# A decode block on one core: one tile program with a rolled load loop, and five engine programs with their own semaphores

## The chip, the cores and the metric

One core of a Trainium2 chip runs the kernel; the other cores have nothing to do with it. The metric is the device time of one execution in microseconds. The profile is one further execution, recorded by the hardware profiler.

## The reference

One token of width 640 passes a transformer block: layer norm, attention over a cache of 8192 positions with 32 heads of width 192, a residual, layer norm again, a gated FFN with ReLU, a residual. All data are 32-bit floats. The two caches are 201 MB each and by far the largest inputs.

```python
def reference(A_x, A_k_cache, A_v_cache, A_wq, A_wo, B_x, B_W_gate, B_W_up, B_W_down):
    # B, Sq, D = 1, 1, 640; H, Sk, Dh = 32, 8192, 192; F = 1536
    q = (layernorm(x) @ wq).reshape(B, Sq, H, Dh).transpose(0, 2, 1, 3)
    p = softmax(einsum("bhqd,bhkd->bhqk", q, k_cache) * (Dh ** -0.5))
    o = einsum("bhqk,bhkd->bhqd", p, v_cache)
    h = x + o.transpose(0, 2, 1, 3).reshape(B, Sq, H * Dh) @ wo
    n = layernorm(h)
    gate = n @ W_gate
    return h + ((gate * (gate > 0)) * (n @ W_up)) @ W_down
```

The excerpt joins the two blocks of the reference and leaves out its helper functions.

## The kernel before

The host packs, for every head, one array of keys (`kq`) and one of values (`vo`), each 128 partitions by 13248 floats, so that one transfer of 6.78 MB brings a head's K with its query weights, and another its V with its output weights. The transfers all go through the load queue that SyncE (SP) feeds.

There is one buffer for K (`kp`, `k_t`) and there are two for V (`vp`, `v_t`). A head is two functions. `keys` computes the head's query with five matmuls from the weights behind K (line 156), picks its components out with two reductions on VectorE (`ttr`, line 148), spreads them over columns with two scalings on ScalarE (lines 164 and 165), and forms the scores with 24 matmuls of 512 columns (line 171), each of which the profile shows as two passes. Then come the maximum (lines 174 to 178), the exponential (line 181) and the reciprocal of its sum (line 185). `values` multiplies V with the probabilities in twelve VectorE instructions of 1024 columns, each with its sum over the row (line 148 again), adds up with TensorE (line 195), scales, and adds the head's part of the output projection to the accumulator `acc` in PSUM, where it stays over all heads (lines 203 and 205).

Thirty heads run in a loop, two heads in each turn (`For_i`, line 213); the last two stand behind it, and the last V comes in four pieces. `manual_schedule` keeps each engine's instructions in the order of the program text: the query of a head stands behind the values of the head before on TensorE, and each wait is derived from the buffers by the tile framework. At the end of the loop the engines meet at a barrier. The FFN's weights go into the K buffer and one V buffer, in the load queue behind the last V (lines 232 to 236). The FFN itself is lines 238 to 287: row sums of the accumulator on ScalarE (242), the statistics, the up and gate projections (266), the ReLU product and its transpose (276, 278), the down projection (283), the residual (286), the store (287).

Of the kernel before, what the change touches and what calls it, by code (L numbers as in the profile page):

```python
# [15 lines left out]
NG = 8  # L16
# [3 lines left out]
QB = 512  # L20
D1 = P
D2 = DH - P
KW = S + S // 2
WW = DH * D // P
TW = KW + WW
# [4 lines left out]
@with_exitstack  # L30
def kernel(
    ctx: ExitStack,
    tc: tile.TileContext,
    x: bass.AP,
    kq: bass.AP,
    vo: bass.AP,
    w_gate: bass.AP,
    w_up: bass.AP,
    w_down: bass.AP,
    out: bass.AP,  # L40
):
    nc = tc.nc
    DG = D // NQ
    FG = F // NQ

    const = ctx.enter_context(tc.tile_pool(name="const", bufs=1))
    kp = ctx.enter_context(tc.tile_pool(name="kp", bufs=1))
    vp = ctx.enter_context(tc.tile_pool(name="vp", bufs=2))
    pp = ctx.enter_context(tc.tile_pool(name="pp", bufs=2))
    small = ctx.enter_context(tc.tile_pool(name="small", bufs=2))  # L50
    row = ctx.enter_context(tc.tile_pool(name="row", bufs=1))
    ps_s = ctx.enter_context(tc.tile_pool(name="ps_s", bufs=1, space=bass.MemoryType.PSUM))
    ps_q = ctx.enter_context(tc.tile_pool(name="ps_q", bufs=2, space=bass.MemoryType.PSUM))
    ps_m = ctx.enter_context(tc.tile_pool(name="ps_m", bufs=2, space=bass.MemoryType.PSUM))
    ps_a = ctx.enter_context(tc.tile_pool(name="ps_a", bufs=1, space=bass.MemoryType.PSUM))
    ctx.enter_context(tc.manual_schedule())

    xT = const.tile([P, DJ], F32, name="xT")
    nc.sync.dma_start(xT, x[0, 0].rearrange("(p j) -> p j", p=P))

    def load_k(h):
        t = kp.tile([P, TW], F32, name="k_t")
        nc.sync.dma_start(t, kq[h])
        return t

    def load_v(h, parts):
        t = vp.tile([P, TW], F32, name="v_t")
        b = 0
        for n in parts:
            nc.sync.dma_start(t[:, b:b + n], vo[h][:, b:b + n])  # L70
            b += n
        return t

    xrow = const.tile([1, D], F32, name="xrow")
    nc.scalar.dma_start(xrow, x[0])

    ones = const.tile([P, P], F32, name="ones")
    nc.gpsimd.memset(ones, 1.0)
    share = const.tile([P, P], F32, name="share")
    nc.gpsimd.memset(share, 1.0 / C)  # L80
    eps = const.tile([P, 1], F32, name="eps")
    nc.gpsimd.memset(eps, EPS)
    ident = const.tile([P, P], F32, name="ident")
    from concourse.masks import make_identity
    make_identity(nc, ident)

    def fold(name, n, view):
        t = const.tile([P, n], F32, name=name)
        nc.vector.reduce_sum(t, view, axis=AX.X)
        return t  # L90

    low = fold("low", D2, ident.rearrange("p (a f) -> p f a", f=D2))
    same = const.tile([P, NG, C], F32, name="same")
    nc.vector.reduce_sum(same[:, 0, :], ident.rearrange("p (a c) -> p c a", c=C), axis=AX.X)
    nc.vector.tensor_copy(same[:, 1:NG, :], same[:, 0:1, :].to_broadcast([P, NG - 1, C]))
    blk = fold("blk", NG, ident.rearrange("p (a c) -> p a c", c=C))
    blk2 = fold("blk2", NJ - NG, low.rearrange("p (a c) -> p a c", c=C))
    half = fold("half", 2, ident.rearrange("p (a c) -> p a c", c=D2))
    side = const.tile([P, 2, D2], F32, name="side")
    nc.vector.tensor_copy(side, half[:, :, None].to_broadcast([P, 2, D2]))  # L100
    pick = const.tile([P, 3, 2, C], F32, name="pick")
    nc.gpsimd.memset(pick, 0.0)
    for i in range(2):
        nc.gpsimd.memset(pick[:, i, i, :], 1.0)
    nc.vector.tensor_copy(pick[:, 2], half[:, :, None].to_broadcast([P, 2, C]))

    def rstd_of(dst, var, name):

        ve = const.tile([P, 1], F32, name=f"ve{name}")
        nc.vector.tensor_scalar_add(ve, var, EPS)  # L110
        sd = const.tile([P, 1], F32, name=f"sd{name}")
        nc.scalar.activation(sd, var, AF.Sqrt, bias=eps)
        y = const.tile([P, 1], F32, name=f"y{name}")
        nc.vector.reciprocal(y, sd)
        t = const.tile([P, 1], F32, name=f"t{name}")
        nc.vector.scalar_tensor_tensor(t, y, ve, y, op0=ALU.mult, op1=ALU.mult)
        nc.vector.tensor_scalar(t, t, -0.5, 1.5, op0=ALU.mult, op1=ALU.add)
        nc.vector.tensor_mul(dst, y, t)

    s1 = const.tile([P, 1], F32, name="s1")  # L120
    nc.vector.reduce_sum(s1, xT, axis=AX.X)
    pm = ps_m.tile([P, QB], F32, name="ps_small")
    nc.tensor.matmul(pm[:, 0:1], ones, s1, start=True, stop=True)
    mean = const.tile([P, 1], F32, name="mean")
    nc.vector.tensor_scalar_mul(mean, pm[:, 0:1], 1.0 / D)
    xc = const.tile([P, DJ], F32, name="xc")
    nc.vector.tensor_scalar(xc, xT, mean, None, op0=ALU.subtract)
    xsq = const.tile([P, DJ], F32, name="xsq")
    nc.vector.tensor_mul(xsq, xc, xc)
    s2 = const.tile([P, 1], F32, name="s2")  # L130
    nc.vector.reduce_sum(s2, xsq, axis=AX.X)
    pv = ps_m.tile([P, QB], F32, name="ps_small")
    nc.tensor.matmul(pv[:, 0:1], ones, s2, start=True, stop=True)
    var = const.tile([P, 1], F32, name="var")
    nc.vector.tensor_scalar_mul(var, pv[:, 0:1], 1.0 / D)
    rstd = const.tile([P, 1], F32, name="rstd")
    rstd_of(rstd, var, "x")
    xn = const.tile([P, DJ], F32, name="xn")
    nc.vector.tensor_scalar_mul(xn, xc, rstd)

    HN = D // 2
    acc = ps_a.tile([P, HN], F32, name="acc")
    for i in range(2):
        nc.tensor.matmul(acc[i * D2:(i + 1) * D2, :], ones[0:1, 0:D2], xrow[:, i * HN:(i + 1) * HN],
                         start=True, stop=False, skip_group_check=True)

    def ttr(dst, a, b, scale, out):
        nc.vector.tensor_tensor_reduce(out=out, in0=a, in1=b, scale=scale, scalar=0.0,  # L148
                                       op0=ALU.mult, op1=ALU.add, accum_out=dst)

    def keys(kt):

        wq = kt[:, KW:TW].rearrange("p (j n) -> p j n", n=DH)
        pq = ps_q.tile([P, QB], F32, name="pq")
        for j in range(DJ):
            nc.tensor.matmul(pq[:, 0:DH], xn[:, j:j + 1].to_broadcast([P, P]), wq[:, j, :],  # L156
                             start=(j == 0), stop=(j == DJ - 1))
        q = small.tile([P, 2], F32, name="q")
        junk = small.tile([P, DH], F32, name="junk")
        ttr(q[:, 0:1], ident, pq[:, 0:D1], SCALE, junk[:, 0:D1])  # L160
        ttr(q[:, 1:2], low, pq[:, D1:DH], SCALE, junk[:, D1:DH])
        qs = small.tile([P, 3, 2 * C], F32, name="qs")
        pk = pick.rearrange("p i a c -> p i (a c)")
        nc.scalar.mul(qs[:, 0:2, :], pk[:, 0:2, :], q[:, 0:1])  # L164
        nc.scalar.mul(qs[:, 2, :], pk[:, 2, :], q[:, 1:2])
        sp = ps_s.tile([P, SG], F32, name="sp")
        for u in range(0, SG, QB):
            for i in range(3):
                for g in range(NQ):
                    c0 = (2 * g + i) * SG + u if i < 2 else S + g * SG + u  # L170
                    nc.tensor.matmul(sp[g * Q:(g + 1) * Q, u:u + QB], qs[:, i, :], kt[:, c0:c0 + QB],  # L171
                                     start=(i == 0), stop=(i == 2))
        mp = small.tile([P, 1], F32, name="mp")
        nc.vector.reduce_max(mp, sp, axis=AX.X)  # L174
        pt = ps_m.tile([P, QB], F32, name="ps_small")
        nc.tensor.transpose(pt[:, 0:P], mp.to_broadcast([P, P]), ident)  # L176
        m1 = small.tile([P, 1], F32, name="m1")
        nc.vector.reduce_max(m1, pt[:, 0:P], axis=AX.X, negate=True)  # L178
        p = pp.tile([P, SG], F32, name="p")
        rs = small.tile([P, 1], F32, name="rs")  # L180
        nc.scalar.activation(p, sp, AF.Exp, bias=m1, accum_out=rs)  # L181
        pl = ps_m.tile([P, QB], F32, name="ps_small")
        nc.tensor.matmul(pl[:, 0:1], share, rs, start=True, stop=True)  # L183
        rl = small.tile([P, 1], F32, name="rl")
        nc.vector.reciprocal(rl, pl[:, 0:1])  # L185
        return p, rl
# [144 lines left out]
```

## Time and profile before

| | us |
|---|---|
| median of three runs | 1108.31 (1103.39 to 1110.35) |
| the profiled execution | 1108.53 |
| its span, first to last instruction | 1105.8 |
| load queue, packets' share of 16 DMA engines | 94.9% |
| VectorE / TensorE busy | 48% / 39% |
| bytes read | 445.91 MB, 403 GB/s over the span |

The span is what the profile divides up; the 2.7 us beside it belong to the execution but to no instruction of the program. A share of busy time is a mean over stages: a queue at 94.9% can be full most of the time and stand still for one stretch. Which stretch that is, the view of windows tells; why, the timeline and the waits.

### The profile page before, as it was taken

What the parts mean: (1) busy time and instruction counts of PE and PEld (TensorE: products, weight loads), DVE (VectorE), ACT (ScalarE), POOL (GpSimd) and SP (SyncE); (2) the same over time, 40 slices, a digit from 0 to 9 for tenths busy, and PEclk for the clock granted to TensorE, in tenths of its full rate; (3) what the DMA queues carried; (4) which work ended last, traced back from release to release, by engine and by line L of the source; (5) the groups of instructions that cost most, each with busy time, mean ns of one, the idle gap of its engine ahead of it and who ended that gap; (6) DMA issues with size and microseconds to landing.
All of it is one profiled execution on the core that took longest, in us unless ns stands there. A gap on an engine that the chain in (4) does not pass through costs nothing. (4 is left out here: it accounts for less than half of the span.)

```text
span 1105.8 us, 7451 instructions
## 1 busy us (share of the span) xinstructions
PE 436.2 (39%) x2396; PEld 213.8 (19%) x2396; DVE 531.4 (48%) x1154; ACT 95.7 (9%) x190; POOL 1.3 (0%) x12
## 2 busy tenths in 40 slices
PE   2345433344443334444333444433344442332346
PEld 1022221112221112222111222211122221111123
DVE  1543455544355554435555443555534455550552
ACT  0101000010101001010100101010010101000101
POOL 0000000000000000000000000000000000000000
PEclk9766656666665666666566666666666666665667
DMA  8999999999999999999999999999999999948995
GB/s 338 399 420 406 429 431 397 433 397 426 399 435 439 395 435 408 427 403 433 427 401 427 403 429 401 447 424 408 429 406 418 406 426 429 404 186 337 400 428 245
DMA packets 10960, 445.99 MB, mean 403 GB/s; under 512 B 1349, under 2 KB 1353, under 8 KB 1866
## 3 DMA queue, kind: packets, MB, share of 16 engines
q1 hardware_dynamic: 10952, 445.92, 94.9%
q8 instruction: 3, 0.05, 0.0%
q14 instruction: 3, 0.02, 0.0%
q10 hardware_dynamic: 2, 0.00, 0.0%
HBM read 445.91 MB, written 0.00 MB: 403 GB/s over the span
## 5 line engine op out<-in xcount | busy, mean ns | idle before, releaser
L148 DVE CUSTOM_DVE_ANT_0 v_t<-v_t,p 128x1024 f32<-128x1024 f32 x384 | 442.5, 1220 | 9.4 <-DMA v_t<-in_vo_dram 8.5
L171 PE MATMUL sp<-k_t,qs 128*32 128x512 f32 x1536 | 199.6, 675 | 48.5 <-ACT qs L164 48.5
L195 PE MATMUL ps_small<-op,same 128*128 128x12 f32 x64 | 19.2, 378 | 460.4 <-DVE op L148 460.4
L174 DVE TENSOR_REDUCE mp<-sp 128x1 f32<-128x1024 f32 x32 | 39.2, 1225 | 235.4 <-PE sp L171 235.4
L156 PE MATMUL pq<-k_t,xn 128*128 128x192 f32 x320 | 95.6, 476 | 36.5 <-DMA k_t<-in_kq_dram 36.5
L148 DVE CUSTOM_DVE_ANT_0 junk<-ident,pq 128x128 f32<-128x128 f32 x32 | 9.2, 288 | 208.1 <-PE pq L156 208.1
L195 PEld LDWEIGHTS ps_small<-op,same 128*128 128x128 f32 x64 | 16.0, 311 | 463.1 <-DVE op L148 463.1
L156 PEld LDWEIGHTS pq<-k_t,xn 128*128 128x128 f32 x320 | 95.2, 313 | 50.2 <-issue 49.8
L171 PEld LDWEIGHTS sp<-k_t,qs 128*32 128x32 f32 x1536 | 52.0, 121 | 177.4 <-issue 118.5
L181 ACT ACTIVATE p<-sp,m 128x1024 f32<-128x1024 f32 x32 | 35.7, 1114 | 265.6 <-DVE m L178 265.6
L201 ACT ACTIVATE o<-side,o 128x128 f32<-128x128 f32 x32 | 12.9, 402 | 512.4 <-DVE o L148 512.4
L203 PE MATMUL acc<-v_t,o 128*64 128x320 f32 x128 | 42.7, 768 | 10.4 <-DVE o L148 10.4
L205 PE MATMUL acc<-v_t,o 128*128 128x320 f32 x64 | 45.9, 821 | 0.0
L183 PE MATMUL ps_small<-rs,share 128*128 128x1 f32 x64 | 15.1, 306 | 53.7 <-ACT p L181 53.7
L185 DVE RECIPROCAL rl<-ps_small 128x1 f32<-128x1 f32 x32 | 5.4, 168 | 59.5 <-PE ps_small L183 59.5
L148 DVE DVE_READ_ACCUMULATOR2_ANT op<- 128x1 f32 x384 | 31.3, 81 | 0.0
L164 ACT ACT_TABLE_LOAD x16 | 20.5, 1283 | 119.1 <-DVE q L148 119.1
L176 PE MATMUL ps_small<-ident,mp 128*128 128x128 f32 x32 | 9.9, 308 | 47.8 <-DVE mp L174 47.8
L183 PEld LDWEIGHTS ps_small<-rs,share 128*128 128x128 f32 x64 | 12.4, 241 | 59.8 <-ACT p L181 59.8
L148 DVE CUSTOM_DVE_ANT_0 junk<-blk,ps_small,rl 128x8 f32<-128x8 f32 x64 | 11.6, 218 | 22.2 <-PE ps_small L195 22.2
L205 PEld LDWEIGHTS acc<-v_t,o 128*128 128x128 f32 x64 | 16.1, 313 | 31.0 <-ACT o L201 31.0
L176 PEld LDWEIGHTS ps_small<-ident,mp 128*128 128x128 f32 x32 | 4.3, 133 | 76.3 <-issue 39.1
(79 smaller groups left out, 104.6 us busy)
## 6 DMA issues: line engine op xcount, KB each, us to landing
k_t<-in_kq_dram SPq DMA_DIRECT2D x32, 6624.0 KB, 20.2
v_t<-in_vo_dram SPq DMA_DIRECT2D x31, 6624.0 KB, 35.2
v_t<-in_vo_dram SPq DMA_DIRECT2D x3, 1536.0 KB, 27.2
ffn_a<-in_w_up_dram SPq DMA_DIRECT2D x1, 3840.0 KB
ffn_a<-in_w_gate_dram SPq DMA_DIRECT2D x1, 2304.0 KB, 20.1
v_t<-in_vo_dram SPq DMA_DIRECT2D x1, 2016.0 KB
ffn_b<-in_w_down_dram SPq DMA_DIRECT2D x1, 1920.0 KB, 27.4
ffn_b<-in_w_gate_dram SPq DMA_DIRECT2D x1, 1536.0 KB, 23.2
```

The source lines that it names most:

```text
L148: nc.vector.tensor_tensor_reduce(out=out, in0=a, in1=b, scale=scale, scalar=0.0, op0=ALU.mult, op1=ALU.add, accum_out=dst)
L156: nc.tensor.matmul(pq[:, 0:DH], xn[:, j:j + 1].to_broadcast([P, P]), wq[:, j, :], start=(j == 0), stop=(j == DJ - 1))
L164: nc.scalar.mul(qs[:, 0:2, :], pk[:, 0:2, :], q[:, 0:1])
L171: nc.tensor.matmul(sp[g * Q:(g + 1) * Q, u:u + QB], qs[:, i, :], kt[:, c0:c0 + QB], start=(i == 0), stop=(i == 2))
L174: nc.vector.reduce_max(mp, sp, axis=AX.X)
L176: nc.tensor.transpose(pt[:, 0:P], mp.to_broadcast([P, P]), ident)
L181: nc.scalar.activation(p, sp, AF.Exp, bias=m1, accum_out=rs)
L183: nc.tensor.matmul(pl[:, 0:1], share, rs, start=True, stop=True)
L195: nc.tensor.matmul(po[:, 0:NJ], same.rearrange("p a c -> p (a c)"), op, start=True, stop=True)
L201: nc.scalar.mul(o2, side.rearrange("p a c -> p (a c)"), o[:, 1:2])
L203: nc.tensor.matmul(acc[i * D2:(i + 1) * D2, :], o[:, 0:1].to_broadcast([P, D2]), vt[:, KW + i * HN:KW + (i + 1) * HN], start=False, stop=F ...
L205: nc.tensor.matmul(acc, o2, vt[:, KW + D:TW], start=False, stop=last, skip_group_check=True)
```

## The change

The tile framework is gone. Five functions hold the programs of the five engines, every wait and every increment of a semaphore is written out, and all buffers are single allocations: two for V, one of everything else.

- SP runs a straight list of transfers for all 32 heads with a wait ahead of each: K of a head waits for the scores of the head before (`sp`), V for the output sums of two heads before (`wo`).
- The query weights of a head lie behind V of the head before. The first head's come in a transfer of their own, with x (`w0`, 0.49 MB). K is 128 x 12288 floats then, V 128 x 14208.
- TensorE, VectorE and ScalarE each have a loop over two heads, from 1 to 32. In a turn TensorE does the scores of head n, then the sums and the output part of head n - 1 (`output`), then the small matmuls of head n's softmax, then the query of head n + 1, behind a wait for V. VectorE combines head n - 1, finds the maximum, multiplies V, and between the sixth and the seventh product reduces the query of head n + 1 (`columns`). The first `output` works on zeros; the last `query`, `columns` and `masks` work for a head that is not there.
- K is stored by halves of the score columns, the last K comes in two pieces, the last V in four.
- The FFN's up weights and four of the five gate rows go into a V buffer, the rest into the K buffer (three rows and two before).

The new head order, from the changed kernel (statistics, FFN and set-up left out; they compute what they did):

```python
    def sync_fn(sy):
        sy.dma_start(wq0, w0).then_inc(s["w0"], 16)
        sy.sem_inc(s["k2"], 16 * (H - 1))
        for n in ("vb1", "vb2", "vb3"):
            sy.sem_inc(s[n], 16 * (H // 2 - 1))
        for h in range(H):
            if h > 0:
                sy.wait_ge(s["sp"], h)
            if h < H - 1:
                sy.dma_start(kt, kk[h]).then_inc(s["k"], 16)
            else:
                sy.dma_start(kt[:, 0:KW // 2], kk[h][:, 0:KW // 2]).then_inc(s["k"], 16)
                sy.dma_start(kt[:, KW // 2:KW], kk[h][:, KW // 2:KW]).then_inc(s["k2"], 16)
            if h > 0:
                sy.wait_ge(s["wo"], h)
            if h < H - 1:
                sy.dma_start(vts[h % 2], vv[h]).then_inc(s["vb" if h % 2 else "va"], 16)
            else:
                W = JV * SG
                for i, n in enumerate(("vb", "vb1", "vb2", "vb3")):
                    c0, c1 = i * W, (i + 1) * W if i < 3 else KW + WO
                    sy.dma_start(vts[1][:, c0:c1], v0[:, c0:c1]).then_inc(s[n], 16)
        sy.wait_ge(s["wo"], H)
        for i, (dst, src, n) in enumerate(ffn):
            if i == 2:
                sy.wait_ge(s["sp"], H)
            sy.dma_start(dst, src).then_inc(s[n], 16)
        sy.wait_ge(s["o4"], 1)
        sy.dma_start(out[0].rearrange("o (g n) -> (o g) n", g=NQ), o4[0:P:Q, :]).then_inc(s["out"], 16)
        sy.wait_ge(s["out"], 16)
...
        def columns(n):
            v.wait_ge(s["q"], n)
            ttr(v, q[:, 0:1], ident, pq[:, 0:D1], SCALE, junk[:, 0:D1])
            ttr(v, q[:, 1:2], low, pq[:, D1:DH], SCALE, junk[:, D1:DH]).then_inc(s["qd"])

        def combine(n):
            v.wait_ge(s["po"], n)
            ttr(v, o[:, 0:1], blk, po[:, 0:NG], rl, junk2[:, 0:NG])
            ttr(v, o[:, 1:2], blk2, po[:, NG:NJ], rl, junk2[:, NG:NJ]).then_inc(s["o"])

        def head(i, b, i8):
            n = i + b if b else i
            combine(n)
            v.wait_ge(s["sp"], n)
            v.reduce_max(mp, sp, axis=AX.X).then_inc(s["mp"])
            v.wait_ge(s["pt"], n)
            v.reduce_max(m1, pt[:, 0:P], axis=AX.X, negate=True).then_inc(s["m1"])
            v.wait_ge(s["pl"], n)
            v.reciprocal(rl, pl[:, 0:1])
            vt = vts[b]
            v.wait_ge(s["vb" if b else "va"], i8)
            for j in range(NJ):
                if b and j and j % JV == 0:
                    v.wait_ge(s[f"vb{j // JV}"], i8)
                if j == NJ // 2:
                    columns(n + 1)
                blkj = vt[:, j * SG:(j + 1) * SG]
                ins = ttr(v, op[:, j:j + 1], blkj, p, 1.0, blkj)
            ins.then_inc(s["op"])

        columns(1)
        with v.Fori(1, H + 1, 2) as i:
            i8 = i * 8 + 8
            head(i, 0, i8)
            head(i, 1, i8)
        combine(H + 1)
...
        def masks(n):
            a.wait_ge(s["qd"], n)
            pk = pick.rearrange("p i a c -> p i (a c)")
            a.mul(qs[:, 0:2, :], pk[:, 0:2, :], q[:, 0:1])
            a.mul(qs[:, 2, :], pk[:, 2, :], q[:, 1:2]).then_inc(s["qs"])

        def second(n):
            a.wait_ge(s["o"], n)
            a.mul(o2, side.rearrange("p a c -> p (a c)"), o[:, 1:2]).then_inc(s["o2"])

        def head(n):
            second(n)
            a.wait_ge(s["m1"], n)
            a.activation(p, sp, AF.Exp, bias=m1, accum_out=rs).then_inc(s["rs"])
            masks(n + 1)

        masks(1)
        with a.Fori(1, H + 1, 2) as i:
            head(i)
            head(i + 1)
        second(H + 1)
...
        def query(w):
            wq = w.rearrange("p (j n) -> p j n", n=DH)
            for j in range(DJ):
                ins = mm(pq[:, 0:DH], xn[:, j:j + 1].to_broadcast([P, P]), wq[:, j, :], j == 0, j == DJ - 1)
            ins.then_inc(s["q"])

        def scores():
            for u in range(NU):
                if u:
                    yield
                for k in range(3):
                    for g in range(NQ):
                        c0 = u * (KW // 2) + (k * NQ + g) * QB
                        ins = mm(sp[g * Q:(g + 1) * Q, u * QB:(u + 1) * QB], qs[:, k, :], kt[:, c0:c0 + QB],
                                 k == 0, k == 2)
            ins.then_inc(s["sp"])
            yield

        def output(n, vt):
            t.wait_ge(s["op"], n)
            mm(po[:, 0:NJ], same.rearrange("p a c -> p (a c)"), op, True, True).then_inc(s["po"])
            t.wait_ge(s["o"], n)
            for i in range(2):
                mm(acc[i * D2:(i + 1) * D2, 0:HN], o[:, 0:1].to_broadcast([P, D2]),
                   vt[:, KW + i * HN:KW + (i + 1) * HN], False, False, skip_group_check=True)
            t.wait_ge(s["o2"], n)
            mm(acc[:, 0:HN], o2, vt[:, KW + D:KW + WO], False, False, skip_group_check=True).then_inc(s["wo"])

        def head(i, b, i8):
            n = i + b if b else i
            t.wait_ge(s["qs"], n)
            sc = scores()
            k_wait(i, b, "k")
            next(sc)
            k_wait(i, b, "k2")
            next(sc)
            output(n, vts[1 - b])
            t.wait_ge(s["mp"], n)
            t.transpose(pt[:, 0:P], mp.to_broadcast([P, P]), ident).then_inc(s["pt"])
            t.wait_ge(s["rs"], n)
            mm(pl[:, 0:1], share, rs, True, True).then_inc(s["pl"])
            t.wait_ge(s["vb3" if b else "va"], i8)
            if b:
                t.wait_ge(s["vb"], i8)
            query(vts[b][:, KW + WO:VW])

        def k_wait(i, b, name):
            t.wait_ge(s[name], i * 16 + 16 * b if b else i * 16)
...
        query(wq0[:, 0:WQ])
        with t.Fori(1, H + 1, 2) as i:
            i8 = i * 8 + 8
            head(i, 0, i8)
            head(i, 1, i8)
        output(H + 1, vts[1])
```

The edit of the call and of the packing:

```diff
-    kq = _np.empty((H, P, TW), k.dtype)
-    vo = _np.empty((H, P, TW), v.dtype)
+    kk = _np.empty((H, P, KW), k.dtype)
+    vv = _np.empty((H - 1, P, VW), v.dtype)
+    v0 = _np.empty((P, KW + WO), v.dtype)
+    w0 = _np.empty((P, WQ + DJ), v.dtype)
...
+        if h < H - 1:
+            r[:, KW + WO:] = w[:, :, h + 1, :].reshape(P, WQ)
...
-    with _tile.TileContext(nc) as tc:
-        tile_mha_decode_reglu_kernel(tc, *args)
+    with nc.cleanup_on_exit():
+        mha_decode_reglu_kernel(nc, *args)
```

More of the change, by code (lines that the diff above doesn't have):

```diff
@@ L20 @@
 QB = 512
+NU = SG // QB
 D1 = P
 D2 = DH - P
+DG, FG, HN = D // NQ, F // NQ, D // 2
 KW = S + S // 2
[L24 to L25 removed]
+WO = D + HN
+WQ = DJ * DH
+VW = KW + WO + WQ
+JV = 3
+JA = 4
+JB = 6
 SCALE = DH ** -0.5
 EPS = 1e-5
[L30 to L186, printed above, removed]
[L188 to L220 removed]
@@ L278 @@
-    nc.vector.transpose(guT, gu.rearrange("p (c j) -> p j c", c=Q))
-    pd = ps_m.tile([P, QB], F32, name="ps_small")
-    for j in range(FJ):
-        for g in range(NQ):
-            nc.tensor.matmul(pd[g * Q:(g + 1) * Q, 0:DG], guT[:, j, :], dn[:, j, g * DG:(g + 1) * DG],
-                             start=(j == 0), stop=(j == FJ - 1))
-    o4 = row.tile([P, DG], F32, name="o4")
-    nc.vector.scalar_tensor_tensor(o4, pd[:, 0:DG], hr, h4, op0=ALU.mult, op1=ALU.add)
-    nc.sync.dma_start(out[0].rearrange("o (g n) -> (o g) n", g=NQ), o4[0:P:Q, :])
@@ new lines, in pool_fn @@
+    def pool_fn(g):
+        c = Chain(nc, g, "e_pool")
+        c(g.memset(ones, 1.0))
+        c(g.memset(share, 1.0 / C))
+        c(g.memset(eps, EPS))
+        c(g.memset(pick, 0.0))
+        c(g.memset(op, 0.0))
+        c(g.memset(rl, 1.0))
+        c(g.memset(vts[1][:, KW:KW + WO], 0.0))
+        c(g.memset(ident, 0.0))
+        c.sync()
+        c(g.affine_select(out=ident, in_=ident, compare_op=ALU.not_equal, fill=1.0, base=0,
+                          pattern=[[-1, P]], channel_multiplier=1))
+        for i in range(2):
+            c(g.memset(pick[:, i, i, :], 1.0))
+        c.sync()
+        g.sem_inc(s["cst"], 1)
```

315 lines of the change are left out of this document (222 added, 93 removed).

## The prediction

> **What bounds the kernel now.** I read the page's shares first, then cut the span into its stages.
>
> ```profile
> span 1105.8 us, 7451 instructions
> PE 436.2 (39%) x2396; PEld 213.8 (19%) x2396; DVE 531.4 (48%) x1154; ACT 95.7 (9%) x190; POOL 1.3 (0%) x12
> q1 hardware_dynamic: 10952, 445.92, 94.9%
> HBM read 445.91 MB, written 0.00 MB: 403 GB/s over the span
> ```
>
> No engine is busy for half of the span; the load queue's packets fill 94.9% of it. So this is a streaming kernel, and its time is bytes over rate plus every microsecond without a transfer. The view of windows says where those are (columns: stretch, its length, busy time of the engines, granted PE clock, DMA share, GB/s).
>
> ```profile
> 302.00:360.00 58.00, 21.15 (x105) 10.87 (x108) 31.22 (x68) 4.41 (x9) 0.00 (x0) 0.62 1.01 433
> 332.00:362.00 30.00, 11.05 (x56) 5.31 (x60) 14.89 (x33) 2.68 (x6) 0.00 (x0) 0.60 1.00 433
> 949.00:979.00 30.00, 11.91 (x68) 6.16 (x68) 16.11 (x35) 2.17 (x5) 0.00 (x0) 0.66 0.99 429
> 360.00:364.00 4.00, 3.67 (x36) 0.84 (x28) 0.12 (x1) 0.00 (x0) 0.00 (x0) 1.00 0.61 265
> 0.00:6.10 6.10, 1.60 (x6) 1.29 (x8) 2.74 (x15) 0.18 (x1) 1.30 (x12) 1.00 0.01 1
> 6.10:980.50 974.40, 389.75 (x2064) 190.73 (x2060) 477.68 (x1026) 84.52 (x165) 0.00 (x0) 0.67 0.98 418
> 980.50:1000.60 20.10, 3.89 (x10) 1.80 (x10) 14.38 (x29) 1.14 (x3) 0.00 (x0) 0.52 0.00 0
> 1000.60:1096.00 95.40, 35.93 (x206) 16.63 (x210) 34.82 (x81) 9.86 (x23) 0.00 (x0) 0.62 0.97 409
> 1096.00:1105.80 9.80, 5.01 (x116) 3.38 (x108) 1.78 (x3) 0.00 (x0) 0.00 (x0) 1.00 0.00 0
> ```
>
> The reader is to see five stages: 6.1 us before the first byte; the loop of 30 heads at 418 GB/s; 20.1 us with no transfer at all; the last two heads with the FFN weights at 409; 9.8 us after the last byte. Where the queue never runs dry (the first three rows) it goes at 429 to 433; the row at 360 shows the dip that costs the loop its mean. The timeline of one head names the cause.
>
> ```profile
> 316.21 0.08 DVE L148 DVE_READ_ACCUMULATOR2_ANT op<- 128x1 f32 x1
> ...
> 319.76 3.11 PE L156 MATMUL pq<-k_t,xn 128*128 128x192 f32 x10
> ...
> 322.91 0.29 DVE L148 CUSTOM_DVE_ANT_0 junk<-ident,pq 128x128 f32<-128x128 f32 x1 [5.56 <-PE pq L156]
> ...
> 323.31 0.35 ACT L164 ACTIVATE qs<-pick,q 128x64 f32<-128x64 f32 x1 [5.45 <-DVE q L148]
> ...
> 323.70 5.36 PE L171 MATMUL sp<-k_t,qs 128*32 128x512 f32 x48 [0.83 <-ACT qs L164]
> ...
> 329.20 0.33 SPq L63 DMA_DIRECT2D k_t<-in_kq_dram  x1
> ...
> 332.96 0.17 DVE L185 RECIPROCAL rl<-ps_small 128x1 f32<-128x1 f32 x1 [1.82 <-PE ps_small L183]
> ...
> 334.96 1.22 DVE L148 CUSTOM_DVE_ANT_0 v_t<-v_t,p 128x1024 f32<-128x1024 f32 x1 [1.83 <-DMA v_t<-in_vo_dram]
> ...
> 356.71 6.96 PE L171 MATMUL sp<-k_t,qs 128*32 128x512 f32 x48 [2.21 <-ACT qs L164]
> ...
> 363.82 0.33 SPq L63 DMA_DIRECT2D k_t<-in_kq_dram  x1
> ```
>
> There is one key buffer, so the next K is issued when the scores have been read out of it. And the scores come late: PE runs them behind the query, the query behind the preceding head's values (ended 316.21). In the head at 329.20 that is just in time; in the other it is at 363.82, when the queue has been dry for over a microsecond. The wait list of the load queue has the same releaser:
>
> ```profile
> SPq L63 <- PE sp L171: 376.0, 30, 14.2
> ```
>
> **The change part by part.** *The head's order.* Scores of 48 matmuls no longer wait for a query computed from K's own tile. By the code K is now 128 x 12288 floats, 6.29 MB, 14.5 us at 433; V with output weights and the next head's query weights is 7.27 MB, 16.8 us; a head is 31.3 us. Count from the landing of V at T. PE does the query (3.1 us, row at 319.76). DVE does six of its twelve products,
>
> ```profile
> L148 DVE CUSTOM_DVE_ANT_0 v_t<-v_t,p 128x1024 f32<-128x1024 f32 x384 | 442.5, 1220 | 9.4 <-DMA v_t<-in_vo_dram 8.5
> ```
>
> 6 x 1.15 us as they overlap (the chain of the tail below starts one each 1.14), so 6.9; then the two reductions of q and the two scalings (322.91 to 323.70, 0.8). The mask is there at T + 7.7, the next K lands at T + 14.5, so the scores start at the landing. They take 5.4 to 8.2 us, the longest being the first head's:
>
> ```profile
> 24.22 3.54 PE L156 MATMUL pq<-k_t,xn 128*128 128x192 f32 x10 [17.32 <-DMA k_t<-in_kq_dram]
> ...
> 29.98 8.19 PE L171 MATMUL sp<-k_t,qs 128*32 128x512 f32 x48 [2.22 <-ACT qs L164]
> ```
>
> So K is issued at the latest at T + 22.8, with 0.1 us from scores to issue (329.06 to 329.20), and V keeps the queue fed until T + 31.3. From this go 1.0 us from issue to data (K issued at 5.15 below, bytes from 6.1) and the lag of the last of the 16 DMA engines: the first K, 6.78 MB, should be in at 6.1 + 15.7 = 21.8 and frees PE at 24.2, so 2.4. Left: 5 us of cover. The dips are gone; with that cover used up, each further microsecond of late scores would cost 32 us over the heads. The V load waits for the output sums of two heads back, 3.7 us after the scores (1080.14 to 1083.85 in the tail's chain, below), while K itself streams for 14.5: hidden too. What is late next is nothing on an engine: DVE's cycle from values to values. Its products end at T + 14.5, the scores at the latest at T + 22.7; sums (3.7) and then transpose, exponential and reciprocal (scores' end 329.06 to 333.13, less 1.2 for the maximum that runs beside the sums, 2.9) end it at T + 29.3, still under 31.3.
>
> *The straight load list.* SP has no loop, so the barrier behind the two-head loop no longer holds it:
>
> ```profile
> 0.75 0.40 SPq L59 DMA_DIRECT2D xT<-in_x_dram  x1
> 5.15 0.36 SPq L63 DMA_DIRECT2D k_t<-in_kq_dram  x1
> ...
> 947.84 0.33 SPq L70 DMA_DIRECT2D v_t<-in_vo_dram  x1
> 1000.63 0.34 SPq L63 DMA_DIRECT2D k_t<-in_kq_dram  x1
> ```
>
> The 20.1 us between 980.5 and 1000.6 go. At the start the first load can issue at 0.75 instead of 5.15, so bytes flow from about 1.8. The new first load (query weights of head 0 and x, 0.49 MB, 1.1 us) only moves bytes; layer norm and query then end at about 15 us, under K's load until 18.
>
> *The stream.* Total bytes stay 445.9 MB; 11.8 of them are the FFN's, at the end. Ahead of these are 434.1 MB: at 433, 1002.6 us. Per-transfer restarts and the lag of the last engine are not shown for a queue that is never dry, so I bound them: 0 (row at 302) to 36 us (434.1 MB at the loop's 418 is 1038.5). I take 4, which is 431 GB/s, between the rows of 433 and 429, since these are the stretches without a dip. Last V in at 1.8 + 1002.6 + 4 = 1008.4.
>
> The HBM Reference of the Trainium skill (Specifications) has a core streaming alone at about 425 GB/s, bounded by its DMA engines. The trace holds 433 for 58 us, so the measurement decides here; by 425 the stream would be 1021 us and the kernel some 15 us slower than my sum.
>
> *The tail.* K of the last head comes in two pieces, V in four, as V did before. But the loop body computes a query for a 33rd head. DVE stands at that query's reductions after six products, PE's query waits for the last piece of V. So from the last landing L: query 3.2, reductions 0.5, six products 6.9, in all 10.6 to the last product. From there the chain is the old one:
>
> ```profile
> 1053.16 3.21 PE pq L156 x10
> ...
> 1080.14 0.02 DVE op L148
> ...
> 1082.47 1.38 PE acc L205 x2
> ...
> 1088.08 6.24 PE pu L266 x40
> 1094.32 3.28 PE pg L266 x40
> ...
> 1099.18 3.51 PE ps_small L283 x96
> ...
> 1102.72 0.38 DVE o L286
> ```
>
> 1080.14 to the end at 1105.8 is 25.7 us. L + 36.3. The FFN weights, 11.8 MB or 27.2 us, are in at about L + 28; the down projection starts 19.0 us behind the last product, at L + 29.6, so they are covered by under 2 us. Own semaphores for DVE's small steps in start and tail: 0 to 1 us, taken as 0, because the stretches between such steps in the old chain are already waits. The other ways of dividing buffers (single p, gate rows 4 and 1 instead of 3 and 2) move no byte on the path; single buffers are hidden by DVE's own order.
>
> *Sum.* 1008.4 + 36.3 = 1044.7 us span against 1105.8. The profiled execution took 1108.53, 2.7 more than its span, and stands 0.2 above the median 1108.31. Kept: 1047.4, so 1047 to 1048.
>
> **The rivals.** *The loop's rate is not the dips'.* If 418 is what long streams give, the change keeps only the exit, the start and the tail: 1.8 + 1038.5 + 36.3 + 2.7 = 1079. For it: 418 over 974 us. Against: 433 over 58 us with transfers queued.
>
> *A fuller queue is slower.* The stretch from 1000.6 had the most transfers queued and ran at 409; 434.1 MB at that rate are 1061, the sum 1102, within 1%. Against: the stretch holds its own dip after the restart, and the FFN's small pieces.
>
> *Slower: the V load stuck behind its own wait.* SP waits for the output sums, then issues V; the next K is queued behind that. Output sums need the last product of the head before. Should they come after K has landed, the queue runs dry in each head by the difference. It decides from 14.5 us after the K issue, and the kernel is slower than before from 2 us per head on (61 saved over 32 heads). If PE's order put the sums behind a whole value phase, 14.2 us after the scores and 3.7 more, it is 17.9, a loss of 3.4 + 1.0 + 2.4 lag = 6.8 each: 1048 + 32 x 6.8 = 1266. Against: by the count above the products end at T + 15, ahead of the scores' end, so the sums come 3.7 us after the K issue. A wait read wrongly by me is what would bring it about.
>
> **How the numbers follow.** Forecast 0.84, first rival 0.08, second 0.03, slower one 0.05. Range: below, no restarts, 2 us less tail and 1 less start, 1041, set to 1040; above, half of the 36 us bound on restarts instead of 4, 1062, and up to 4 us of FFN weights out of cover, 1066. That leaves the rivals' 0.16 out. Faster by over 1% (about what a measurement of this kernel can tell from no change) has the first two cases, 0.92; within 1% 0.03; slower 0.05.
>
> **What would show it.** DMA at 428 or more in every slice but the first and last, no slice near 186; each K issued 5 to 9 us after the one before has landed, and DVE's first product of a head waiting for the V load; first load before 1 us; DVE idle before the last head's query reductions for some 3 us; the last product 10 to 12 us behind the last V piece. Wrong would be me, if SP's waits were for the output sums longer than 6 us, if the packets' share stayed at 95%, or if windows with transfers queued showed under 425 GB/s.

## The result and the profile after

The changed kernel takes 1045.65 us (median of four runs, 1045.39 to 1046.43), the one before 1105.88 us on the same chip: a ratio of 0.945, with a 95% interval of 0.942 to 0.949. The forecast was 1047 to 1048. These are the rows of the page after that answer to those quoted of before (in the third row are the GB/s of each fortieth of the span):

```profile
span 1043.8 us, 6624 instructions
PE 453.8 (43%) x2414; PEld 209.0 (20%) x2414; DVE 525.5 (50%) x1162; ACT 77.6 (7%) x179; POOL 2.1 (0%) x15
GB/s 397 445 423 429 433 448 422 444 423 431 431 448 422 444 423 429 431 448 424 444 421 431 431 446 424 441 426 431 431 443 426 441 426 431 431 443 426 421 429 247
q1 hardware_dynamic: 11096, 445.92, 99.0%
```

The bytes are the same (445.92 MB) and the packets now fill 99.0% of the span instead of 94.9%. ScalarE (ACT) has lost 18 us of work, 95.7 to 77.6; I had passed over that row, and it is half of the story below. The view of windows, with columns as before:

```profile
0.00:1.80 1.80, 0.00 (x0) 0.00 (x0) 0.00 (x0) 0.50 (x1) 1.27 (x11) 1.00 0.08 12
1.80:980.50 978.70, 422.08 (x2157) 194.68 (x2157) 494.45 (x1088) 69.77 (x159) 0.86 (x5) 0.65 1.00 433
980.50:1008.00 27.50, 11.30 (x61) 3.76 (x62) 19.31 (x41) 2.17 (x5) 0.00 (x0) 0.69 1.01 431
1008.00:1035.00 27.00, 16.51 (x102) 7.55 (x100) 9.93 (x31) 5.20 (x15) 0.00 (x0) 0.62 0.93 390
1035.00:1043.80 8.80, 3.95 (x104) 3.02 (x96) 1.78 (x3) 0.00 (x0) 0.00 (x0) 1.00 0.00 0
```

The loop's 418 GB/s has become 433 over 979 us, the stretch without a transfer is gone, and the lead-in is 1.8 us instead of 6.1. The 62.0 us of span that went can be laid out by these rows. The loop moved 418 x 974.4 = 407 MB, which takes 940.6 us at 433: 33.8. The stop at the loop's exit: 20.1. The start: 6.1 less 1.8, so 4.3. The remainder, 3.8, lies in the last two heads and the tail.

The HBM Reference of the Trainium skill (Specifications), with its 425 GB/s for a core alone, is below what is held here, and the kernel did not come out the 15 us slower that the prediction worked out from it; the measurement decides.

One head in the middle, from the timeline (start, busy time, engine and line, operation, idle time before it and what ended that):

```profile
302.21 8.29 PE L330 MATMUL sp<-kt,qs 128*32 128x512 f32 x48 [10.96 <-DMA kt<-in_kk_dram]
310.57 0.33 SPq L147 DMA_DIRECT2D kt<-in_kk_dram  x1
318.99 1.22 DVE L135 CUSTOM_DVE_ANT_0 vt<-vt,p 128x1024 f32<-128x1024 f32 x1 [3.89 <-DMA vt<-in_vv_dram]
319.10 3.54 PE L330 MATMUL pq<-vt,xn 128*128 128x192 f32 x10 [4.21 <-DMA vt<-in_vv_dram]
326.59 0.30 ACT L299 ACTIVATE qs<-pick,q 128x32 f32<-128x32 f32 x1
333.54 7.99 PE L330 MATMUL sp<-kt,qs 128*32 128x512 f32 x48 [10.90 <-DMA kt<-in_kk_dram]
```

PE and DVE both stand and wait for the loads. The mask (326.59) is ready 6.6 us before the K it serves, scores start at K's landing, and the next K is issued 8.36 us later. The V that was then streaming lands at 318.99, so the queue still had 8.4 us of work at that issue.

### The profile page after: what moved, and what is told of

Its sections match the earlier page's. It is cut to its first block, busy times and chain, and to the rows that moved or that the text cites. A ratio compares the mean times of both kernels' runs of the same rounds, so it can differ in the third digit from the quotient of the medians.

```text
span 1043.8 us, 6624 instructions
## 1 busy us (share of the span) xinstructions
PE 453.8 (43%) x2414; PEld 209.0 (20%) x2414; DVE 525.5 (50%) x1162; ACT 77.6 (7%) x179; POOL 2.1 (0%) x15
## 3 DMA queue, kind: packets, MB, share of 16 engines
q1 hardware_dynamic: 11096, 445.92, 99.0%
## 4 chain that ended last, share of the span: by engine, by line
DMA 73%; PE 25%; DVE 1%; issue 0%; ACT 0%; SPq 0%; DVEq 0%
DMA kt<-in_kk_dram 70%; PE sp L330 23%; DMA vt<-in_v_dram 4%; PE pq L330 1%; DVE vt L135 1%; PE acc L330 0%; ACT h L320 0%; SPq L159 0%; DVE junk L135 0%; PE po L330 0%; DVE guT L284 0%; PE pt L330 0%; DVE gu L283 0%; PE pl L330 0%; SPq L139 0%
## 5 line engine op out<-in xcount | busy, mean ns | idle before, releaser
L135 DVE CUSTOM_DVE_ANT_0 vt<-vt,p 128x1024 f32<-128x1024 f32 x384 | 444.9, 1221 | 142.1 <-DMA vt<-in_vv_dram 142.1
L330 PE MATMUL sp<-kt,qs 128*32 128x512 f32 x1536 | 239.7, 789 | 342.1 <-DMA kt<-in_kk_dram 337.6
L330 PE MATMUL pq<-vt,xn 128*128 128x192 f32 x320 | 113.1, 539 | 159.0 <-DMA vt<-in_vv_dram 150.5
L330 PEld LDWEIGHTS sp<-kt,qs 128*32 128x32 f32 x1536 | 55.8, 140 | 512.6 <-DMA kt<-in_kk_dram 359.4
L330 PEld LDWEIGHTS pq<-vt,xn 128*128 128x128 f32 x320 | 97.9, 331 | 161.3 <-DMA vt<-in_vv_dram 78.8
L330 PE MATMUL acc<-vt,o 128*64 128x320 f32 (+1 forms) x198 | 50.5, 476 | 15.3 <-DVE o L135 15.3
L330 PE MATMUL pl<-rs,share 128*128 128x1 f32 x64 | 16.0, 319 | 51.9 <-ACT p L308 51.9
L330 PEld LDWEIGHTS pl<-rs,share 128*128 128x128 f32 x64 | 13.3, 258 | 62.6 <-ACT p L308 62.6
L330 PEld LDWEIGHTS acc<-vt,o 128*64 128x64 f32 (+1 forms) x198 | 16.6, 154 | 35.1 <-DVE o L135 18.4
L330 PE MATMUL po<-op,same 128*128 128x12 f32 x66 | 13.1, 273 | 7.4 <-DVE op L135 7.4
L299 ACT ACTIVATE qs<-pick,q 128x32 f32<-128x32 f32 x33 | 10.1, 307 | 0.0
```

The source lines that it names most:

```text
L135: return eng.tensor_tensor_reduce(out=res, in0=a, in1=b, scale=scale, scalar=0.0, op0=ALU.mult, op1=ALU.add, accum_out=dst)
L299: a.mul(qs[:, 2, :], pk[:, 2, :], q[:, 1:2]).then_inc(s["qs"])
L330: return t.matmul(dst, lhsT, rhs, start=start, stop=stop, **kw)
```

## The experiments

Two explanations of the loop's 34 us stood against each other. Mine: the scores came late because PE had to do the preceding head's values and the query ahead of them, and moving the query is what cured it. The rival came from a row of the kernel before that I had not read:

```profile
L164 ACT ACT_TABLE_LOAD x16 | 20.5, 1283 | 119.1 <-DVE q L148 119.1
```

The first Exp in the kernel stood inside the loop, behind the square root of the norm; so ScalarE loaded its function table again in each of the 15 turns of two heads and once more behind the loop, 16 times in all, just ahead of the mask for which the scores wait.

**Undo the loop alone** (before, its head loop written out):

```diff
-    with tc.For_i(0, H - 2, 2, hint_engines=(), iteration_sync="reg_based") as i:
-        head(i, [TW])
-        head(i + 1, [TW])
+    for i in range(H - 2):
+        head(i, [TW])
```

> The kernel before with its two-head loop written out as 30 single heads; nothing else is changed, so the query stays behind K, and in the head order behind the values of the head before. The barrier at the loop's end (20.1 us without a transfer) and the wait at its start (K issued at 5.15 us) are gone, and so are the 15 reloads of the activation table that ScalarE did in the loop (1.28 us each, ahead of the scaling of the mask). Theory (stages add up; the dips come where scores are later than the V load ahead of them, which in this kernel is the head with the table reload): about 1.8 + 1003 + 4 to 12 + 38.2 + 2.7 = 1050 to 1058 us. Rival (the query's place is what makes the dips, and moving it is what ended them): only exit and start go, 1106 - 20 - 4 = 1082 us, and stretches of the stream stay near 418 GB/s.

Measured 1056.05 us, ratio 0.954 (0.952 to 0.956), inside the range named: some five sixths of the change's gain, with the query still in K's path.

```profile
0.00:2.20 2.20, 0.00 (x0) 0.00 (x0) 0.56 (x2) 0.00 (x0) 1.29 (x12) 1.00 0.03 2
2.20:980.00 977.80, 378.40 (x2136) 190.77 (x2136) 494.11 (x1074) 68.40 (x155) 0.00 (x0) 0.67 1.00 429
```

Stop and late start went with the loop, as they should. But the rate rose to 429 as well. Written out, the kernel has one table load for all heads instead of 16, and that is the only difference on a head's path that I find. The scores of the heads that had the load now start 0.83 us behind PE's last work and take the short time, the eleventh head's for instance:

```profile
344.32 5.36 PE L171 MATMUL sp<-k_t,qs 128*32 128x512 f32 x48 [0.83 <-ACT qs L164]
```

**Take away the table load alone** (before, with one unused Exp of a single element ahead of the loop):

```diff
+    warm = const.tile([1, 1], F32, name="warm")
+    nc.scalar.activation(warm, eps[0:1, :], AF.Exp)
```

> The kernel before with one exponential of a single element ahead of the loop, so that the loop starts with the table it needs and no longer reloads it in every turn. The loop, its barrier and the query's place stay. Theory (a dip of 1 to 2 us in every second head, in the head with the reload): the 1.28 us off that head's path take away most of its dip, 15 turns x 1.0 to 1.3 us = 15 to 20 us off: 1086 to 1091 us. Rival (dips from the query's place alone, the reload hidden in the wait): within 4 us of 1106.

Measured 1076.09 us, 0.973 (0.971 to 0.975). One added instruction gains 30 us, half of the whole change; I had expected 15 to 20. The windows and a second head of before (first two fences) and of this kernel (third and fourth):

```profile
355.02 1.28 ACT L164 ACT_TABLE_LOAD   x1 [4.67 <-DVE q L148]
```

```profile
353.00:356.70 3.70, 1.50 (x9) 1.21 (x7) 0.52 (x4) 1.67 (x3) 0.00 (x0) 0.96 1.06 458
356.70:359.70 3.00, 2.99 (x16) 0.79 (x20) 0.00 (x0) 0.17 (x1) 0.00 (x0) 0.50 1.14 495
359.70:363.10 3.40, 3.40 (x36) 0.84 (x28) 0.00 (x0) 0.00 (x0) 0.00 (x0) 0.96 0.72 312
```

```profile
345.18 5.36 PE L174 MATMUL sp<-k_t,qs 128*32 128x512 f32 x48 [0.93 <-ACT qs L167]
350.68 0.33 SPq L63 DMA_DIRECT2D k_t<-in_kq_dram  x1
```

```profile
6.10:940.00 933.90, 355.53 (x2015) 181.28 (x2011) 476.02 (x1023) 65.72 (x149) 0.00 (x0) 0.67 1.00 432
345.10:350.70 5.60, 5.36 (x48) 1.46 (x48) 0.00 (x0) 0.24 (x2) 0.00 (x0) 1.00 1.05 454
```

Read the PE clock in before's three windows: 0.96, then 0.50 for 3 us, then 0.96. The 1.28 us of table load leave PE without a matmul for 2.21 us; behind that the scores' first 3 us run at a granted clock of 0.50 and take 6.96 us instead of 5.36. Load and slow matmuls together make K's issue 2.9 us late in every second head (1.28 + 1.60), and the queue runs short: 312 GB/s in the third window. Without the load the wait is 0.93, the clock stays at 1.00, the rate at 432.

"TensorE: Matmul & The Clock Gate" of the Trainium skill (Part 1, the HAM clock gate) has the half clock follow an idle window of about 3.4 us that runs freely; here a wait of 2.2 us was enough, in all 16 heads with a table load.

**Is it the table or the lateness?** (the kernel with the early Exp, and in each turn's first head an activation whose result nothing uses, ahead of the mask)

```diff
+        if delay:
+            nc.scalar.activation(slow2, slow, AF.Copy, scale=q[:, 1:2])
```

> The kernel before without the table reload in its loop (as in the run with the exponential ahead of the loop), but with one plain activation of 128x1024 (1.1 us) in its place: in the first head of each turn, behind the reductions of the query and ahead of the scalings. Its result is not used. Theory (what costs is that the scores come late, whatever makes them late): back to near the kernel before, 1095 to 1106 us. Rival (the table reload does something of its own, for instance to the transfers): stays at 1076 to 1080 us.

Measured 1105.22 us against before, 0.999 (0.997 to 1.001): everything is given back.

```profile
L171 ACT ACTIVATE slow<-slow,q 128x1024 f32<-128x1024 f32 x15 | 17.2, 1147 | 93.2 <-DVE q L154 93.2
```

```profile
96.44 5.36 PE L179 MATMUL sp<-k_t,qs 128*32 128x512 f32 x48 [2.20 <-ACT qs L172]
...
353.38 7.05 PE L179 MATMUL sp<-k_t,qs 128*32 128x512 f32 x48 [2.20 <-ACT qs L172]
```

```profile
6.10:940.00 933.90, 362.79 (x1958) 178.33 (x1958) 459.81 (x989) 79.67 (x161) 0.00 (x0) 0.67 0.99 419
```

There is no table load in this loop, and 1.15 us of plain work in 15 turns does the same: PE waits 2.20, the scores take 7 us in 12 of the 15 heads, the rate falls to 419. So a table load is not costly as such; what costs is a delay between q and mask, whatever makes it. The half clock does not follow from the wait alone: in the other three heads, the one at 96.44 among them, the scores take 5.36 us behind the same wait.

**Table loads in the changed kernel** (one-element Sqrt and Exp, results unused, ahead of each mask):

```diff
+            a.activation(dm[:, 0:1], eps[0:1, :], AF.Sqrt)
+            a.activation(dm[:, 1:2], eps[0:1, :], AF.Exp)
```

> The changed kernel with two one-element activations (a square root and an exponential) ahead of the scalings in every head, so that ScalarE loads its table twice there: 2 x 1.28 us and two small activations, some 3 us more on the way from query to mask in each head. The kernel before lost 30 us to half a reload of that kind per head. Theory (the mask is ready some 6 us ahead of the landing of K): nothing, 1045 to 1047 us. Rival (ScalarE's path is the limit here as there): 32 x 2 to 3 us, 1110 to 1140 us.

Measured 1044.96 us against 1045.08 for the changed kernel on that chip. Groups by line and the loop's window:

```profile
L299 ACT ACT_TABLE_LOAD x33 | 42.3, 1283 | 0.6
L300 ACT ACT_TABLE_LOAD x33 | 42.3, 1283 | 0.2
```

```profile
6.00:980.00 974.00, 419.91 (x2155) 193.85 (x2151) 492.07 (x1078) 158.89 (x283) 0.00 (x0) 0.65 1.00 433
```

66 loads of 1283 ns, 85 us of ScalarE, cost nothing. Only one of the two in each head lies on the way from query to mask; the other ran before q was there, while ScalarE had nothing to do. So the mask comes 1.6 us later and not the 3 us that I had named:

```profile
326.29 1.28 ACT L300 ACT_TABLE_LOAD   x1
```

In this head it is ready at 328.23, still 5.1 us before its K, for which the scores wait until 333.29. The page "ScalarE: Activation LUTs" of the Trainium skill (What ACT_TABLE_LOAD costs) gives 1283 ns for a load too. The 16 loads of the kernel before cost it 30 us and these 66 nothing, by their place alone.

**Put the query back into K's path** (the changed kernel with each head's query weights behind its own K, and query, reductions and mask between landing and scores):

```diff
-            t.wait_ge(s["qs"], n)
             sc = scores()
             k_wait(i, b, "k")
-            next(sc)
             k_wait(i, b, "k2")
+            query(kt[:, KW:TK])
+            t.wait_ge(s["qs"], n)
+            next(sc)
...
-            query(vts[b][:, KW + WO:VW])
```

> The changed kernel with one part undone: each head's query weights lie behind its own K again (K 6.78 MB, V 6.78 MB), and the query, its reductions and the scalings run between the landing of K and the scores. Side effects: the first load holds only x, the query for a 33rd head is gone, and the FFN's gate rows are divided 3 and 2. Theory: query 3.6 + reductions 0.5 + scalings 0.7 + scores 5.4 to 7.2 put the K issue 10.2 to 12.0 us behind the landing of K; V lasts 15.7 us less 1.0 from issue to data and 1.8 of lag between the engines, 12.9: the stream stays full by 1 to 3 us, and the tail is some 3 us shorter without the 33rd query: 1041 to 1047 us. Rival (the query has to be out of K's path or the dips are back): 31 heads x 1 to 1.5 us more, 1073 to 1090 us.

Measured 1063.92 us, 0.961 (0.959 to 0.963): 18 us of the change's 60 are lost again. That is above the theory's range and below the rival's; neither had it. Two heads from the timeline, then the loop's window of this kernel:

```profile
307.02 3.56 PE L328 MATMUL pq<-kt,xn 128*128 128x192 f32 x10 [14.26 <-DMA kt<-in_kk_dram]
...
311.70 7.47 PE L328 MATMUL sp<-kt,qs 128*32 128x512 f32 x48 [1.12 <-ACT qs L298]
319.25 0.33 SPq L148 DMA_DIRECT2D kt<-in_kk_dram  x1
...
339.88 3.57 PE L328 MATMUL pq<-kt,xn 128*128 128x192 f32 x10 [16.11 <-DMA kt<-in_kk_dram]
...
344.57 5.36 PE L328 MATMUL sp<-kt,qs 128*32 128x512 f32 x48 [1.12 <-ACT qs L298]
349.99 0.33 SPq L148 DMA_DIRECT2D kt<-in_kk_dram  x1
```

```profile
6.00:980.00 974.00, 375.11 (x2086) 185.72 (x2082) 488.55 (x1064) 67.02 (x154) 0.00 (x0) 0.65 1.00 427
```

The issue comes 12.2 us behind the query's start in one head and 10.1 in the other, against 8.4 at most in the changed kernel. The wait ahead of the scores is 1.12 us in both, yet they take 7.47 and 5.36; they are that slow in 14 of the 32 heads. The loop at 427 instead of 433 costs 974 x 6/433 = 13.5 us, and at the landing of the last K the loss is 17.3 of the span's 18.6 (the first row is of this kernel, the second of the changed one):

```profile
1008.70 3.54 PE L328 MATMUL pq<-kt,xn 128*128 128x192 f32 x10 [16.08 <-DMA kt<-in_kk_dram]
```

```profile
991.43 2.78 PE L330 MATMUL sp<-kt,qs 128*32 128x512 f32 x24 [1.26 <-DMA kt<-in_kk_dram]
```

So nearly all of it is lost in the stream. In the tail the last head's query behind its K is about paid for by the 33rd query that this version leaves out, which by itself is worth 4.5 us (below). Beside the version without it, at 1040.59 us, the query's place is worth some 23 us. So the new place does buy something, three to four tenths of the gain, and not the dips as a whole.

**Restore the stop at the end of the loop** (the changed kernel, one wait ahead of the last but one K):

```diff
+            if h == H - 2:
+                sy.wait_ge(s["op"], h + 1)
```

> The changed kernel with one more wait: the K load of the last head but one waits until VectorE has ended the products of the head before, as it did behind the loop's barrier. Theory: the queue is dry from about 1 us before that head's V has landed until 14.6 us of products and 1.0 us to the first data are over, 16 to 18 us, and nothing downstream gives it back: span 1043.8 + 17 = 1060 to 1062 us. Rival (the stop is hidden, because the FFN weights at the end have slack): under 1050 us.

Measured 1062.65 us in one run, with a span of 1060.6, 16.8 more than the changed kernel's 1043.8. That K is issued at 959.39, and up to then next to nothing flows, as this window shows for 14 us (DMA share 0.02, 8 GB/s):

```profile
942.00:956.00 14.00, 3.54 (x10) 3.06 (x10) 10.89 (x23) 0.56 (x2) 0.00 (x0) 0.62 0.02 8
```

**Restore the late first K** (the changed kernel, first K behind the norm):

```diff
+            else:
+                sy.wait_ge(s["st"], 7)
```

> The changed kernel with the first K load waiting for the layer norm of x (about 10 us) instead of going at 1.45 us. Theory: the stream is the limit from its first byte, so the time without a transfer counts in full, less the 1.1 us of the first small load: 1045 + 7.5 to 9 = 1053 to 1054 us. Rival (the start is hidden by later slack): 1045 us.

Measured 1052.44 us in one run, 6.7 more than the changed kernel's profiled execution (1045.74). The first fence is of the changed kernel, the second of this one:

```profile
0.73 0.40 SPq L139 DMA_DIRECT2D wq<-in_w_dram  x1
1.45 0.33 SPq L147 DMA_DIRECT2D kt<-in_kk_dram  x1
```

```profile
9.09 0.33 SPq L149 DMA_DIRECT2D kt<-in_kk_dram  x1
```

The first K goes 7.64 us late. That a little less than this is lost fits the small first load, which now moves during the wait; how much it takes off was not measured by itself. The time is slightly under the range on record, since the norm was done at 9.0 and not at about 10.

**How much cover is there?** (the changed kernel, each half's scores computed twice, then thrice; the result is that of the last pass)

```diff
+                for _ in range(2):
```

> The changed kernel with the scores of each head computed twice over, which puts the K issue 5.4 us later in each head. Theory: the cover is 5.0 to 7 us, so only the heads with slow scores touch it, 0 to 0.5 us each: 1045 to 1060 us. Computed three times over it lost 133 us over 31 heads, 4.3 each, which with 10.7 us of delay makes a cover of 6.4. Rival (a cost in proportion to the delay, half of the 133): 1110 us.

> The changed kernel with the scores of each head computed three times over (the same results), which puts the K issue 2 x 5.4 = 10.7 us later in each head. Theory: cover is the 8.4 us from the K issue to the landing of V less 1.0 from issue to data and 1.8 to 2.4 of lag between the engines, 5.0 to 5.6 in the heads with slow scores and up to 1.6 more in those with quick ones; 4 to 5.7 us of each head's delay are beyond it, x 31 = 125 to 175 us: 1170 to 1220 us. Rival (scores are on the path already, so that all of the delay counts): 1045 + 31 x 10.7 = 1377 us. Rival (the queue has more slack than I count, or the DMA waits for something else): under 1100 us.

Twice: 1065.57 us, 20 more, where I had put the threshold above it; a miss. Thrice: 1178.93, inside its range. Each is one run. The loop's window and one head's scores, first of the one, then of the other:

```profile
6.00:980.00 974.00, 532.41 (x3526) 204.75 (x3522) 485.53 (x1064) 67.34 (x155) 0.00 (x0) 0.76 0.99 424
308.37 13.37 PE L330 MATMUL sp<-kt,qs 128*32 128x512 f32 x96 [11.04 <-DMA kt<-in_kk_dram]
```

```profile
6.00:980.00 974.00, 629.41 (x4471) 233.16 (x4467) 434.67 (x956) 60.86 (x140) 0.00 (x0) 0.79 0.90 382
303.89 17.42 PE L330 MATMUL sp<-kt,qs 128*32 128x512 f32 x144 [9.98 <-DMA kt<-in_kk_dram]
```

Over the first 31 heads the scores take 7.5 us on average in the changed kernel, 12.6 here and 17.8 there. So 5.1 us more cost 0.65 us a head (20 us over 31), and 10.3 more cost 4.3 (133 over 31). The 5 us of cover are about right, but the edge is soft: the rate falls from 433 to 424 at a DMA share of still 0.99, and between the two runs some 0.7 us is paid for each microsecond of delay.

**Leave out the 33rd query** (the changed kernel, last two heads outside the loops, without the query, reductions and mask whose result nobody uses):

```diff
-            masks(n + 1)
+            if not last:
+                masks(n + 1)
...
+            if last:
+                return
             t.wait_ge(s["vb3" if b else "va"], i8)
```

> The changed kernel with the last two heads written out behind the loops of TensorE, VectorE and ScalarE, and without the query, reductions and scalings for a 33rd head. Theory: the last product comes 3.5 us behind the last piece of V instead of 10.9; the chain to the down projection (19.0 us) is then ready at L + 22.5, before the last FFN weights land at about L + 28, so the weights set the end: last weights at about 1035 + 0.5 for the last matmuls + 0.4 residual + 2.7 to 3.1 for the store = 1039 to 1040 us span, 1041 to 1042 us time. Rival 1 (the chain still sets the end): all 7.4 us come off, 1038 us. Rival 2 (something else sets the tail, the reductions were not the wait): 1045 to 1046 us.

Measured 1040.59 us, ratio 0.941 (0.938 to 0.944), and the changed kernel beside it, run again as a base:

> The changed kernel as it is, for comparison on the same chip. Expected 1045 to 1047 us.

1045.08 us, 0.945 (0.942 to 0.948). So the fastest version is 4.5 us below the change. The time is within a microsecond of the expected one, but not for the expected reason. I thought that the FFN weights would become the end; by the timeline the down projection runs through in 3.47 us without a stop, and the chain shows the last head's own work:

```profile
991.42 4.48 PE sp L335 x24
...
1000.50 1.12 DVE vt L135
...
1014.28 0.62 PE po L335 x2
```

```profile
1032.28 3.47 PE L335 MATMUL pq<-kt,guT 128*32 128x160 f32 x96 [1.65 <-DVE guT L286]
```

The last K piece is in at 991.4, and scores, exponential and twelve products follow each other up to 1014.28. From 1000.50 these are 13.8 us, 1.15 for each product, which is DVE's pace without a wait: it and not V's landing or the weights sets the end.

## Why the prediction was right, and where it was not

*The sum.* Bytes from 1.8 us: so it is. Last V in at 1008.4: 1007.3. Last product 10.6 us behind that: 10.9. From there 25.7: 25.5. Span 1044.7: 1043.8; kept beside it 2.7, measured 1.9. The timeline of the tail:

```profile
1007.34 3.57 PE L330 MATMUL pq<-vt,xn 128*128 128x192 f32 x10 [8.53 <-DMA vt<-in_v_dram]
1010.94 0.29 DVE L135 CUSTOM_DVE_ANT_0 junk<-ident,pq 128x128 f32<-128x128 f32 x1 [5.07 <-PE pq L330]
1018.31 0.60 PE L330 MATMUL po<-op,same 128*128 128x12 f32 x2 [7.41 <-DVE op L135]
```

The query for the 33rd head does hold DVE, for 5.07 us where I said some 3. The two parts with a mechanism of their own, the stop and the start, were confirmed apart from the rest by restoring each, in one run: 16.8 and 6.7 us.

*The loop's rate.* That 418 was dips and not what long streams give is shown: 432 in the kernel before, with one added instruction. The step that failed is what the prediction put ahead of that, "the scores come late: PE runs them behind the query, the query behind the preceding head's values". That order was there in both heads of a turn and is there in the written-out loop too, which streams at 429; of the two heads in the prediction's own fence only the one with the table load had a dip. The two rows that tell it stood there: scores with a wait of 0.83 and 5.36 us, and scores with a wait of 2.21 and 6.96. I explained the lateness by what came before, and never asked why PE waited 1.4 us longer in the second head.

The query's place had used up most of the cover, and the table load overdrew it. In the good head the issue at 329.20 left 5.8 us of V (in at 334.96), by the prediction's own count 2.4 us of cover; the load and the slow scores behind it took 2.9. So either remedy ends these dips: taking the load away with the query left in K's path (432 in the kernel before, though 427 in the changed one), or moving the query with a load left in that path in every head (433). The change has both. My list of parts does not name the second: the changed kernel's code for ScalarE has a one-element Exp behind the norm's square root, ahead of the loop (L293), and so no table load in its loops. The total did not hang on it, since loads in every head left it at 1044.96. What I had wrong is the cause, and with it what the move was needed for.

*The parts of the gain* overlap, so they are not summed: without the loop and its table loads 1056.05, without the table loads alone 1076.09, everything 1045.65. Of the last 10 us, the rate (429 to 433 over 978 us) is 9.

*The cover.* 5 us by the count; issues come 6.8 to 8.4 us behind the landing, within the 5 to 9 named. "With that cover used up, each further microsecond of late scores would cost 32 us" was too sharp: the cost begins at about the cover and is some 0.7 us a head for each further one ((4.3 - 0.65)/5.2), so 22 us over the heads.

*Signs named beforehand.* First load at 0.73, DVE waiting for V in each head, last product 10.9 behind V, packets at 99.0%: as said. "428 or more in every slice" was wrong; between the first and the last they go from 421 to 448, about a mean of 433. Slices of 421 to 424 also are windows with transfers queued under 425 GB/s, which I had named as a sign that I was wrong; slices of 26 us swing too much for such a sign, and the 979 us together hold 433. SP's wait for the output sums, on which the slower rival hung, is 56.8 us over 30 heads, 1.9 at most, from this list of the queue's waits:

```profile
SPq L154 <- PE acc L330: 56.8, 30, 1.9
```

*What stays open.* A K issued 2.9 us late cost 2 us per turn (30 us in 15 turns); how much of that is the dry queue and how much a slow restart was not measured by itself. When PE drops to the half clock is not settled either: a wait of 2.2 us had it behind it in 28 of 31 heads, and one of 1.12 us in 14 of 32. Of the last 10 us between the written-out loop and the change only the query's place was tried by itself, and that in the changed kernel; the price of the scheduler's semaphores against own ones was not.

## What to carry to other kernels

When a stage repeats and only every second turn of it shows a dip, compare the same instruction in a good and in a bad turn, its wait and its duration, before explaining the dip by what both have in common. Look for one-off work that a loop body repeats (here a table load behind a square root), and put one cheap use of it ahead of the loop; then give the load queue a list without barriers and see that what frees a buffer has microseconds to spare, not tenths. An experiment that does one half of a change alone is worth as much when the forecast came true, since two errors or two causes can share a sum.

## What the runs showed of the hardware

Behind a wait of 2.2 us, with a table load or with plain work in it, the scores took some 7 us or more instead of 5.36 in 28 of 31 heads; where the clock was read, it was 0.50 to 0.61 over the first 3 us (0.50 in the window at 356.70). In the loops of the kernel before and of the one with the early Exp a wait of 0.8 to 0.9 us had the short time behind it in every head. A core alone held 433 GB/s for 979 us. And 15 times 1.15 us of work on an engine that is 8% busy cost 29 us (1105.22 against 1076.09), while 66 table loads, 85 us of work on the same engine, cost nothing with 5 us to spare behind them.
